# Softmax totals once per pair, three more folded value loads, and re-cut weight loads of the first MLP, in a two-layer decode kernel

## The chip, the cores and the metric

The kernel runs on one core of a Trainium2 chip. The metric is device time in microseconds (us) of one execution; the lower the better. The core has five engines that run their own instruction streams and wait for one another by semaphores: PE (matmul), DVE (vector), ACT (scalar), POOL (GpSimd) and SP, which here does nothing but issue loads. All loads from device memory run on 16 DMA engines that the whole core shares.

## The reference, cut to what matters

The network is a decode step for two sequences (B = 2) with one token each and D = 576 channels. It applies attention, an MLP, the same attention and the same MLP again, each with a layer norm before it and a residual after it:

```python
x = x + A(layernorm(x)); x = x + M(layernorm(x))
x = x + A(layernorm(x)); x = x + M(layernorm(x))

def A(x):            # 32 heads of 128 channels, 8192 cached positions
    q = (x @ wq)                                   # 576 x 4096
    p = softmax(q . k_cache * 128**-0.5)           # k_cache, v_cache: 2 x 32 x 8192 x 128, f32
    return (p . v_cache) @ wo                      # 4096 x 576
def M(x):            # w_gate, w_up: 576 x 4608; w_down: 4608 x 576
    return (gelu_tanh(x @ w_gate) * (x @ w_up)) @ w_down
```

Each cache holds 268.4 MB, and both attentions read both caches; the weights of one attention and one MLP are 50.7 MB. Almost nothing is computed per byte that is read.

## The kernel before, in words

**Items.** An attention goes through 34 items (`ITEMS`): 30 items of two heads of one sequence (`PAIRS`; items 2k and 2k+1 are the same two heads for sequence 0 and 1), and 4 items of a single head (`SINGLE`). The first attention takes them in order 0 to 33, the second in the opposite order. The keys of an item of two heads are one load of 8.39 MB, its values another. In the steady part of an attention one load of keys and one of values come per item.

**Space.** One tile, `space`, holds everything that is loaded. It has six slots of four parts; an item of two heads takes a pair of slots, so three such loads have a place at a time. Behind and over the last slot lies a ring of four places of 9216 bytes per partition. At build time a small allocator (`Arena`) goes through the program in order: each `done(key)` frees a place, and `pump()` then issues the next loads of one fixed list as far as places are free. So the list sets the order of all loads, SP issues them strictly in that order, and each issue waits at run time for the readers of its place.

**Between the attentions.** Five slots hold keys and values of single-head items over the first MLP, so that the second attention needn't load them (`KEYS_HELD`, `VALUES_HELD`). The first MLP therefore lives on the ring of four places alone: each load there, of 1.18 MB, is issued when PE has read the place. The query weights `wq` of the second attention go through the same ring (`of_half`, `half_products`, L621).

**An item's work.** DVE multiplies keys by the query (L744), POOL adds the halves of each row (L773), DVE adds up the rest (L776). `peak` and `highest` (L798 to L810) find the maximum over all partitions by way of PE, `softmax` (L818) writes weights and per-partition totals on ACT, and `total` (L839) adds the totals over partitions by a matmul with ones, for each item, into one of two small PSUM places that take turns with `highest`; `inverse` (L843) takes reciprocals. `values` (L895) runs the weights against the values on PE, 32 matmuls of 512 columns for an item of two heads. For **folded** items, `folds(n)` (L863), the last two of eight parts are first weighed on DVE (`weigh`, L867, L871 and L876) and added down to four rows on POOL (L879), and one matmul (`folded`, L887) takes the place of eight; this happens while the item after the next is worked on, and frees these two parts only then. `gather`, `context` and `divide` (L934) end a pair of items.

**First MLP.** `norm(split=True)` (L545) writes x transposed in blocks of 32 columns, one block for each two rows of every nine (`u` = 0 to 3) and one for the ninth row. `split_products(h)` (L1112) runs once for each half `h` of the 4608 columns: nine ring places of weights, namely four of gate, one with the ninth rows of gate and up, four of up; each place is 8 matmuls of 288 columns (L1120), which PE's records show as 16 passes. `split_rows` (L272) and `split_middle` (L281) load them; `split_middle` issues two loads of 64 partitions into one place. `activate` (L1142) applies the gate. `down` (L290) loads `w_down` in nine ring places: eight with four rows per partition, and one with the ninth row of four groups in two loads (L305); L1183 multiplies them. The second MLP has room and uses large loads.

**Idle products.** `idle_products(n, side)` (L588, matmul at L592) multiplies the identity with itself into a place that nobody reads. With `side` it writes 256 or 512 columns of one half of the accumulator `acc`; without, 128 columns at a time of a small tile.

**The transition.** `plan_second` (L391) lists the loads of the second attention's start: single parts and groups of parts into places that held data frees one by one (`several_parts`, `one`, `half`; the load is L168).

Of the kernel before, what the change touches and what calls it, by code (L numbers as in the profile page):

```python
# [125 lines left out]
def decode_layers(ctx, tc, x_in, kc, vc, wq, wo, wg, wu, wd, out):  # L126
# [154 lines left out]
    def split_middle(h):  # L281

        def transfers(t):
            for g, w in enumerate((wg, wu)):
                rows = w[:, DF // 2 * h:DF // 2 * (h + 1)].rearrange("(m r) w -> m r w", r=NU)
                nc.sync.dma_start(t[g::2, :], rows[:, NU - 1, :])

        weights(("gu", 0, h), DF // 2, None, transfers)

    def down(layer, piece):  # L290

        src = wd.rearrange("(h p r) c -> p h (r c)", h=2, r=2 * NI)
        apart = wd.rearrange("(t p i) c -> p t i c", t=NT, i=NI)

        def transfers(t):
            if layer == 1:
                h, lo, hi = piece
                nc.sync.dma_start(t, src[:, h, lo * D:hi * D])
            elif len(piece) == 3:
                n, lo, hi = piece  # L300
                nc.sync.dma_start(t.rearrange("p (i c) -> p i c", c=D), apart[:, n, lo:hi, :])
            else:
                to = t.rearrange("p (t c) -> p t c", c=D)
                for lo, hi in ((0, 3), (3, NT)):
                    nc.sync.dma_start(to[:, lo:hi, :], apart[:, lo:hi, NI - 1, :])  # L305

        n = piece[2] - piece[1] if len(piece) == 3 else NT
        weights(("d", layer, piece), n * D, whole_at[layer], transfers)
# [12 lines left out]
    def out_rows(layer, g):  # L321
# [17 lines left out]
        [(t, lo, lo + 4) for t in range(NT) for lo in (0, 4)] + [(NI - 1,)],  # L339
        [(0, 0, 18), (1, 0, 9), (1, 9, 15), (1, 15, 17), (1, 17, 18)],  # L340
# [154 lines left out]
    home = consts.tile([P, 3 * DH + 20], F32, name="home")  # L495
# [19 lines left out]
    smalls = [bank2[:, 4 * GH + P + 2 * i:4 * GH + P + 2 * i + 2] for i in range(2)]  # L515
    low = bank2[:, 4 * GH + P + 4:]
# [20 lines left out]
    def small(p, n):  # L537

        if n > 2:
            return turned[0:p, 0:n]  # L540
        smalls.append(smalls.pop(0))
        return smalls[0][0:p, 0:n]


    def norm(split=False, then=None):  # L545
# [13 lines left out]
        if split:  # L559
            xm = xs[:, :5 * 32].rearrange("p (u m e) -> p u m e", u=5, e=2)  # L560
            nc.vector.tensor_scalar(
                xm[:, 0:4], xr[:, 0:NU - 1, :].rearrange("p (u e) m -> p u m e", e=2), mv[:, 0:1], side[:, 0:1],
                op0=ALU.subtract, op1=ALU.mult,
            )
            to, of_x = xm[:, 4], xr[:, NU - 1, :]
            xs = xs[:, :5 * 32].rearrange("p (u q) -> p u q", u=5)
        else:
            to, of_x = xc, x
            xs = xs.rearrange("p (q u) -> p u q", u=NU)
        nc.vector.scalar_tensor_tensor(  # L570
            to, of_x.unsqueeze(2).to_broadcast(list(to.shape)), mv[:, 0:1],
            side.unsqueeze(1).to_broadcast(list(to.shape)), op0=ALU.subtract, op1=ALU.mult,
        )
# [34 lines left out]
    def attention(layer):  # L608
# [12 lines left out]
        def half_products(h):  # L621

            for k in range(4):
# [6 lines left out]
                if k > 0 if h else k < 3:  # L630
                    idle_products(1)
# [207 lines left out]
        def total(n):  # L839
            tot[n] = small(P, 2)  # L840
            nc.tensor.matmul(tot[n][:, :ITEMS[n].heads], ones, rs.pop(n), start=True, stop=True)  # L841

        def inverse(n):  # L843
            it, t = ITEMS[n], tot.pop(n)
            if it.heads == 2:
                rinv[n] = work.tile([P, 2], F32, name="rinv", bufs=4)
                nc.vector.reciprocal(rinv[n], t)
            else:
                if it.h not in of_head:
                    of_head[it.h] = work.tile([P, 2], F32, name="rinv", bufs=4)  # L850
                rinv[n] = of_head[it.h]
                nc.vector.reciprocal(rinv[n][:, it.b:it.b + 1], t[:, 0:1])
# [10 lines left out]
        def folds(n):  # L863

            return 3 <= n < PAIRS - 3
# [68 lines left out]
        def divide(n, by_scalar=False):  # L934
# [11 lines left out]
            for b, i in ((b, i) for b in range(B) for i in range(2)):  # L946
                to = oT[lo + 32 * i:lo + 32 * i + 32, it.h // GH, :, :, b]
                o = po[lo:lo + 32, :, 2 * b + i:2 * b + i + 1].to_broadcast([32, GH, 2])
                ri = rinv[n - it.b + b][lo:lo + 32, i:i + 1]
# [151 lines left out]
    def mlp(layer):  # L1101
# [10 lines left out]
        def split_products(h):  # L1112

            steps = [(("g", layer, h, u), u, 0) for u in range(4)] + [(("gu", layer, h), 4, 0)]
            steps += [(("u", layer, h, u), u, 1) for u in range(4)]
            for key, u, g in steps:
                w = ready.pop(key).rearrange("p (k c w) -> p k c w", c=4, w=HG)
                for k in range(2):
                    for c in range(4):
                        nc.tensor.matmul(  # L1120
                            acc[32 * c:32 * c + 4 * B, h, :HG], window(u, 4 * k + 2 * g), w[:, k, c, :],
                            start=(key == steps[0][0] and k == 0), stop=(key == steps[-1][0] and k == 1),
                        )
# [47 lines left out]
        for n, piece in enumerate(DOWN[layer]):  # L1171
            if n < len(IDLE[layer]):
                idle_products(IDLE[layer][n], 0)
            w = ready.pop(("d", layer, piece)).rearrange("p (i c) -> p i c", c=D)
            if len(piece) == 1:
                rows = [(t // 2, t % 2, NI - 1) for t in range(NT)]
            elif split:
                rows = [(piece[0] // 2, piece[0] % 2, i) for i in range(piece[1], piece[2])]
            else:
                rows = [(r // NI, piece[0], r % NI) for r in range(piece[1], piece[2])]  # L1180
# [7 lines left out]
            done(("d", layer, piece))  # L1188
# [37 lines left out]
```

## Time and profile before

| | |
|---|---|
| three runs | 2683.21, 2681.78, 2683.00 us; median 2683.0 |
| the profiled execution | 2682.85 us |
| its span, first to last instruction | 2681.1 us |
| busy: PE, DVE, ACT, POOL | 909.0, 1989.8, 165.4, 1551.8 us |
| read from device memory | 1152.39 MB, 430 GB/s over the span |
| chain of work that ended last | DMA 67%, DVE 19%, PE 8%, ACT 3%, POOL 2% |

A busy time is a sum over stages that have different limits, so it doesn't say what a stage is worth. The chain of work is followed back from the last instruction: each piece is what released the next one. A DMA piece of the chain runs from the issue of the load to its landing, so it includes the time that the load spent queued behind earlier loads. A row of the stretches view has start and end of a stretch, its length, the busy time of PE, of PE's weight loads, of DVE, ACT and POOL (in brackets the instructions), the granted PE clock, the busy share of the DMA engines and the rate. A row of the time line has start, duration, engine, line, operation and tiles, and in brackets the idle time before it and who ended it.

### The profile page before, as it was taken

The numbers are of one execution on the slowest core, as the hardware profiler recorded it, in microseconds if no ns is written. First come the engines' busy times: TensorE is split into PE (matmuls) and PEld (weight loads), VectorE is DVE, ScalarE is ACT, GpSimd is POOL, SyncE is SP. The second block draws the span as 40 slices with busy tenths as digits, with TensorE's granted clock in tenths as the row PEclk, the third lists the DMA queues.
The fourth block names the chain that finished last, engine by engine and source line by source line (L and its number), as shares of the span: only waits on it lengthen the run. The fifth ranks groups of instructions, "written<-read, shape, count | busy, mean of one in ns | idle before, by whom it ended". The sixth has DMA issues, their size and how long they took to land.

```text
span 2681.1 us, 15549 instructions
## 1 busy us (share of the span) xinstructions
PE 909.0 (34%) x6276; PEld 284.4 (11%) x6276; DVE 1989.8 (74%) x935; ACT 165.4 (6%) x792; POOL 1551.8 (58%) x407
## 2 busy tenths in 40 slices
PE   1323332233223223334663333223222323332346
PEld 0100000000000000111221100000000000000022
DVE  4878888888788878867037778888888888888740
ACT  0000000000000000001026000000000000000000
POOL 2546676667666766744028457666766666676520
PEclk8656655665566566566986665566566556655678
DMA  9999999999999999999999999999999999999998
GB/s 423 438 430 431 435 434 431 434 432 434 434 432 433 434 432 435 429 430 428 416 411 430 436 429 433 434 434 432 430 436 434 431 434 433 434 432 432 435 428 383
DMA packets 29352, 1153.40 MB, mean 430 GB/s; under 512 B 3272, under 2 KB 3296, under 8 KB 4320
## 3 DMA queue, kind: packets, MB, share of 16 engines
q1 hardware_dynamic: 29240, 1152.40, 99.8%
q8 instruction: 49, 0.80, 0.1%
q14 instruction: 23, 0.19, 0.0%
q10 hardware_dynamic: 40, 0.01, 0.0%
HBM read 1152.39 MB, written 0.00 MB: 430 GB/s over the span
## 4 chain that ended last, share of the span: by engine, by line
DMA 67%; DVE 19%; PE 8%; ACT 3%; POOL 2%; issue 1%; SPq 0%; another core or an unknown queue 0%; POOLq 0%; ACTq 0%; DVEq 0%
DMA space<-in_A_k_cache_dram 57%; DVE space L744 17%; PE acc L887 3%; DMA space<-in_A_v_cache_dram 3%; DMA space<-in_B_w_down_dram 2%; POOL space L773 2%; ACT prz L833 2%; DVE scores L776 2%; PE bank L659 1%; DMA space<-in_B_w_up_dram 1%; DMA space<-in_B_w_gate_dram 1%; PE bank L841 1%; PE bank L810 1%; DMA space<-in_A_wo_dram 1%; ACT space L766 0%
## 5 line engine op out<-in xcount | busy, mean ns | idle before, releaser
L773 POOL TENSOR_TENSOR space<-space 128x3072 f32<-128x3072 f32 (+4 forms) x221 | 1128.0, 5104 | 476.3 <-DVE space L744 331.3
L744 DVE TENSOR_TENSOR space<-space,bank 128x6144 f32<-128x6144 f32 (+4 forms) x223 | 1111.8, 4986 | 343.6 <-DMA space<-in_A_k_cache_dram 270.9
L909 PE MATMUL acc<-space,prz 128*16 128x512 f32 (+1 forms) x3328 | 520.0, 790 | 346.4 <-DMA space<-in_A_v_cache_dram 342.3
L776 DVE TENSOR_REDUCE scores<-space 128x48 f32<-128x3072 f32 (+4 forms) x223 | 569.0, 2551 | 90.8 <-POOL space L773 90.6
L879 POOL TENSOR_TENSOR space<-space 128x2048 f32<-128x2048 f32 x144 | 389.8, 2707 | 384.0 <-DVE space L876 360.7
L659 PE MATMUL bank<-qsb,few 4*64 4x128 f32 (+1 forms) x256 | 46.2, 437 | 889.9 <-DVE space L744 881.9
L876 DVE TENSOR_TENSOR space<-space,bank 128x4096 f32<-128x4096 f32 x48 | 212.2, 4420 | 1.8 <-DVE bank L871 0.2
L909 PEld LDWEIGHTS acc<-space,prz 128*16 128x16 f32 (+1 forms) x3328 | 106.4, 118 | 742.0 <-DMA space<-in_A_v_cache_dram 378.7
L825 ACT ACTIVATE nbs<-bank 128x2 f32<-128x2 f32 (+1 forms) x68 | 11.6, 171 | 2010.2 <-PE bank L810 1973.1
L659 PEld LDWEIGHTS bank<-qsb,few 4*64 4x64 f32 (+1 forms) x256 | 20.8, 202 | 909.9 <-DVE space L744 892.0
L581 POOL TENSOR_TENSOR rstd<-ve,few 128x1 f32<-128x1 f32 x4 | 2.2, 550 | 177.0 <-DVE ve L579 177.0
L887 PE MATMUL acc<-space,few 128*16 128x512 f32 x96 | 90.6, 1047 | 0.0
L802 PE MATMUL bank<-ident,m 128*1 128x128 f32 x68 | 20.3, 298 | 196.3 <-DVE m L800 196.1
L1147 DVE STREAM_TRANSPOSE gu<-acc 128x288 f32<-128x288 f32 x4 | 1.9, 483 | 93.4 <-ACT acc L1145 93.4
L841 PE MATMUL bank<-few 128*128 128x2 f32 x120 | 35.3, 363 | 81.4 <-ACT prz L833 81.4
L932 PE MATMUL bank<-few,wide 128*32 128x4 f32 (+1 forms) x272 | 21.8, 203 | 119.3 <-DVE wide L924 119.3
L833 ACT ACTIVATE prz<-scores,nbs 64x128 f32<-64x128 f32 (+1 forms) x128 | 50.7, 396 | 11.7 <-POOL prz L823 8.8
L766 ACT ACTIVATE space<-space 128x128 f32<-128x128 f32 x164 | 48.4, 296 | 19.8 <-DVE space L744 16.7
L810 PE MATMUL bank<-m,few 1*128 1x2 f32 (+1 forms) x136 | 38.5, 350 | 27.4 <-DVE m L808 27.4
L585 DVE TENSOR_TENSOR x<-bank,x 128x144 f32<-128x144 f32 x4 | 1.2, 308 | 59.1 <-PE bank L1183 39.3
L923 DVE TENSOR_TENSOR acc<-acc,few 128x512 f32<-128x512 f32 x34 | 23.1, 680 | 29.2 <-PE acc L909 29.2
L760 POOL TENSOR_TENSOR space<-space,qs 128x512 f32<-128x512 f32 x23 | 29.2, 1272 | 19.7 <-ACT qs L741 19.7
(103 smaller groups left out, 524.2 us busy)
## 6 DMA issues: line engine op xcount, KB each, us to landing
space<-in_A_k_cache_dram SPq DMA_DIRECT2D x6, 4096.0 KB
space<-in_A_v_cache_dram SPq DMA_DIRECT2D x5, 4096.0 KB
space<-in_B_w_gate_dram SPq DMA_DIRECT2D x8, 1152.0 KB
space<-in_B_w_up_dram SPq DMA_DIRECT2D x8, 1152.0 KB
space<-in_B_w_down_dram SPq DMA_DIRECT2D x8, 1152.0 KB
space<-in_A_wq_dram SPq DMA_DIRECT2D x9, 1024.0 KB
space<-in_A_wo_dram SPq DMA_DIRECT2D x2, 4608.0 KB
space<-in_A_v_cache_dram SPq DMA_DIRECT2D x4, 2048.0 KB
```

Source lines behind the costliest of these rows:

```text
L659: nc.tensor.matmul(qb[n][to, :], pick[32 * c:32 * c + 4, r:r + 1].to_broadcast([4, P // it.heads]), qsb[32 * c:32 * c + 4, (h % 4) * DH:(h ...
L744: nc.vector.tensor_tensor(out=u[:, :r, :], in0=t[:, :r, :], in1=qb[n].unsqueeze(1).to_broadcast([P, r, DH]), op=ALU.mult)
L766: nc.scalar.activation(u[:, j, :], u[:, j, :], AF.Copy, accum_out=S[n][:, base(n, k) + j:base(n, k) + j + 1])
L773: nc.gpsimd.tensor_tensor(out=half, in0=half, in1=u[:, :r, DH // 2:], op=ALU.add)
L776: nc.vector.tensor_reduce(out=S[n][:, base(n, k):base(n, k) + own_rows(n, k, m)], in_=prod.pop((n, k)), axis=AX.X, op=ALU.add)
L810: nc.tensor.matmul(mT[n][:, :heads], ones[0:1, :], m1[:, :heads], start=True, stop=True)
L833: nc.scalar.activation(pr[at, lo:].rearrange("p (g e) -> p g e", e=4)[:, 0:it.rows // 2 * it.heads:2 * it.heads, :], s[at, :it.rows].rearr ...
L841: nc.tensor.matmul(tot[n][:, :ITEMS[n].heads], ones, rs.pop(n), start=True, stop=True)
L876: nc.vector.tensor_tensor(out=t, in0=t, in1=share.unsqueeze(2).to_broadcast([P, rows, DH]), op=ALU.mult)
L879: nc.gpsimd.tensor_tensor(out=t[:, :rows - less], in0=t[:, :rows - less], in1=t[:, less:rows], op=ALU.add)
L887: nc.tensor.matmul(accumulator(n)[0:16, :], owner[:, 8 * ITEMS[n].b:8 * ITEMS[n].b + 16], part_at(arena.live[key, lo][0], 4 * DH), start=F ...
L909: nc.tensor.matmul(accumulator(n)[32 * c:32 * c + m, :], pr[:, at:at + m], t[g // 4][:, g % 4 * 4:g % 4 * 4 + 4, :].rearrange("p j d -> p ...
```

## The change

It does these things at once:

- **Totals.** `total` runs one matmul with four columns once per pair of items, when the second item's totals are there, and `inverse` one reciprocal of four columns. `highest` and `total` each have a PSUM place of their own.
- **Folds.** `folds(n)` holds for `layer < n < 27` in place of `3 <= n < 27`: items 1 and 2 of the first attention and item 2 of the second are folded as well.
- **Ninth rows.** The ninth rows of gate come in one load of 128 partitions (row and half of the columns), those of up in another. Both are used behind the eight other places of half 0, for both halves, with 16 matmuls each; half 1 has eight places. `norm` writes two blocks for the ninth row, one for each half, with zeros between, by a memset on POOL and one more operation on DVE. The columns of a half are now taken with a stride of 18.
- **Down.** The rows of `w_down` are dealt to partitions 18 at a time; eight loads of four rows, and a ninth place with two loads of two rows.
- **Idle products.** In `half_products` one of 512 columns in place of two of 128. In `split_products` one of 256 columns in place of two of 128 for most steps of half 1.
- **Transition.** Two groups of `several_parts` are cut 1 + 3 and 1 + 2 parts in place of 2 + 2 and 2 + 1.

```diff
-    def split_middle(h):
+    def split_ninth(name, w):
+
+        rows = w.rearrange("(m r) (s w) -> m r s w", r=NU, s=2)
...
+            nc.sync.dma_start(t, rows[:, NU - 1, :, :])
+
+        weights((name, 0, 0, NU - 1), DF // 2, None, transfers)
...
-        [(t, lo, lo + 4) for t in range(NT) for lo in (0, 4)] + [(NI - 1,)],
-        [(0, 0, 18), (1, 0, 9), (1, 9, 15), (1, 15, 17), (1, 17, 18)],
+        [[(h, lo, lo + 4)] for h in range(2) for lo in range(0, 16, 4)] + [[(h, 16, 18) for h in range(2)]],
+        [[(0, 0, 18)]] + [[(1, lo, hi)] for lo, hi in ((0, 9), (9, 15), (15, 17), (17, 18))],
...
-        for k in range(0, 4, 2):
-            several_parts(("v", 1, SINGLE[0]), vc, SINGLE[0], k, 2, v63, k)
-        for k, m, where, at in ((1, 2, k62, 0), (3, 2, k62, 2), (5, 2, v62, 0), (7, 1, v62, 2)):
+        for k, m in ((0, 1), (1, 3)):
+            several_parts(("v", 1, SINGLE[0]), vc, SINGLE[0], k, m, v63, k)
+        for k, m, where, at in ((1, 2, k62, 0), (3, 2, k62, 2), (5, 1, v62, 0), (6, 2, v62, 1)):
             several_parts(pair, kc, last, k, m, where, at)
...
                 for u in range(4):
                     split_rows("g", wg, h, u)
-                split_middle(h)
                 for u in range(4):
                     split_rows("u", wu, h, u)
+                if h == 0:
+                    split_ninth("g", wg)
+                    split_ninth("u", wu)
...
+            nc.gpsimd.memset(xs[:, 4 * 32 + 1:4 * 32 + 1 + 2 * 31].rearrange("p (e q) -> p e q", e=2)[:, :, 0:31:2], 0.0)
...
+            own = xs[:, 4 * 32:4 * 32 + 2 * 33].rearrange("p (e q) -> p e q", e=2)[:, :, 0:32:2]
+            nc.vector.tensor_scalar(
+                own, xr[:, NU - 1, :].unsqueeze(1).to_broadcast([P, 2, 16]), mv[:, 0:1], side[:, 0:1],
+                op0=ALU.subtract, op1=ALU.mult,
+            )
+            xs = xs[:, :6 * 32].rearrange("p (u q) -> p u q", u=6)
...
                 if k > 0 if h else k < 3:
-                    idle_products(1)
+                    idle_products(2, 1 - h)
...
         def total(n):
-            tot[n] = small(P, 2)
-            nc.tensor.matmul(tot[n][:, :ITEMS[n].heads], ones, rs.pop(n), start=True, stop=True)
+
+            if ITEMS[n].heads == 1:
+                tot[n] = four[:, 0:1]
+                nc.tensor.matmul(tot[n], ones, rs.pop(n), start=True, stop=True)
+            elif completes(seq.index(n)):
+                tot[n] = four
+                nc.tensor.matmul(tot[n], ones, sums.rearrange("p a i -> p (a i)"), start=True, stop=True)
...
-            return 3 <= n < PAIRS - 3
+            return layer < n < PAIRS - 3
...
-            steps = [(("g", layer, h, u), u, 0) for u in range(4)] + [(("gu", layer, h), 4, 0)]
-            steps += [(("u", layer, h, u), u, 1) for u in range(4)]
+            steps = [((name, layer, h, u), u, g) for g, name in enumerate("gu") for u in range(4)]
+            steps += [((name, layer, h, NU - 1), 4, g) for g, name in enumerate("gu") if h == 0]
             for key, u, g in steps:
-                w = ready.pop(key).rearrange("p (k c w) -> p k c w", c=4, w=HG)
+                w = ready.pop(key).rearrange("p (c m k i) -> p k c m i", c=4, k=2, i=NI)
+                for v in range(2) if u == 4 else (h,):
...
                 if key != steps[-1][0]:
-                    idle_products(1, None if h else 1)
+                    idle_products(1, 1 - h if (u < 4 if h == 0 else u) else None)
```

More of the change, by code (lines that the diff above doesn't have):

```diff
@@ L514, in decode_layers @@
     turned = bank2[:, 4 * GH:4 * GH + P]
-    smalls = [bank2[:, 4 * GH + P + 2 * i:4 * GH + P + 2 * i + 2] for i in range(2)]
-    low = bank2[:, 4 * GH + P + 4:]
+    pair, four = bank2[:, 4 * GH + P:4 * GH + P + 2], bank2[:, 4 * GH + P + 2:4 * GH + P + 6]
+    low = bank2[:, 4 * GH + P + 6:]
     share = low[:, :FOLD * JC]
@@ L1112, in split_products @@
         def split_products(h):
-            steps = [(("g", layer, h, u), u, 0) for u in range(4)] + [(("gu", layer, h), 4, 0)]
-            steps += [(("u", layer, h, u), u, 1) for u in range(4)]
+            steps = [((name, layer, h, u), u, g) for g, name in enumerate("gu") for u in range(4)]
+            steps += [((name, layer, h, NU - 1), 4, g) for g, name in enumerate("gu") if h == 0]
             for key, u, g in steps:
-                w = ready.pop(key).rearrange("p (k c w) -> p k c w", c=4, w=HG)
[L1118 to L1123, printed above, removed]
+                w = ready.pop(key).rearrange("p (c m k i) -> p k c m i", c=4, k=2, i=NI)
+                for v in range(2) if u == 4 else (h,):
+                    for k in range(2):
+                        for c in range(4):
+                            nc.tensor.matmul(
+                                acc[32 * c:32 * c + 4 * B, v, :HG], window(u + (v if u == 4 else 0), 4 * k + 2 * g), w[:, k, c],
+                                start=(k == 0 and (key == steps[0][0] if v == h == 0 else u == 4 and g == 0)),
+                                stop=(key == steps[-1][0] and v == h and k == 1),
+                            )
                 done(key)
                 if key != steps[-1][0]:
-                    idle_products(1, None if h else 1)
+                    idle_products(1, 1 - h if (u < 4 if h == 0 else u) else None)
         def all_products():
@@ L1173, in mlp @@
                 idle_products(IDLE[layer][n], 0)
[L1174 to L1180, printed above, removed]
+            w = ready.pop(("d", layer, piece[0])).rearrange("p (i c) -> p i c", c=D)
+            rows = [(h, *divmod(r, NI)) for h, lo, hi in piece for r in range(lo, hi)]
+            if not split:
+                rows = [(v, h, i) for h, v, i in rows]
             for k, (v, e, i) in enumerate(rows):
```

61 lines of the change are left out of this document (23 added, 38 removed).

## The prediction

> **What bounds the kernel now.** I read the page first, then the rates by stretch, then the chain that ended last.
>
> ```profile
> span 2681.1 us, 15549 instructions
> DMA  9999999999999999999999999999999999999998
> GB/s 423 438 430 431 435 434 431 434 432 434 434 432 433 434 432 435 429 430 428 416 411 430 436 429 433 434 434 432 430 436 434 431 434 433 434 432 432 435 428 383
> q1 hardware_dynamic: 29240, 1152.40, 99.8%
> ```
>
> The DMA engines are busy in every fortieth of the span but the last, at 99.8% of it. The bytes stay the same in the change, 1152.40 MB. At 433 GB/s they take 2661.4 us of the 2681.1; the other 20 us are the start, the tail, and the slices around the first MLP (416 and 411). So the change can act in three ways only: raise the rate in a stretch, leave the DMA engines without a load, or move the tail. The stretches:
>
> ```profile
> 600.00:1000.00 400.00, 116.79 (x630) 32.75 (x630) 327.33 (x122) 16.72 (x70) 268.76 (x63) 0.59 1.00 433
> 1312.00:1318.00 6.00, 2.73 (x34) 0.85 (x34) 0.25 (x1) 0.47 (x1) 0.00 (x0) 1.00 1.01 422
> 1318.00:1326.00 8.00, 6.96 (x60) 2.72 (x60) 1.40 (x8) 0.23 (x1) 0.00 (x0) 0.57 1.01 416
> 1359.00:1366.00 7.00, 4.81 (x86) 2.14 (x84) 0.00 (x0) 0.00 (x0) 0.00 (x0) 1.00 1.03 409
> 1376.00:1390.00 14.00, 11.64 (x68) 3.62 (x69) 5.94 (x4) 3.55 (x19) 3.33 (x3) 0.63 1.01 401
> 1404.00:1410.00 6.00, 1.59 (x14) 0.40 (x6) 5.06 (x6) 5.37 (x36) 6.00 (x6) 1.00 0.95 351
> 1424.00:1452.00 28.00, 16.38 (x106) 4.90 (x97) 23.74 (x27) 19.64 (x129) 22.21 (x17) 0.76 1.01 431
> ```
>
> The steady attention runs at 433 with DVE and POOL idle a fifth and a third of the time. The first MLP, whose runs are of 9216 bytes, reaches 422 where nothing is in its way. Against 422, 1318 to 1326 loses 0.11 us (8 x 6/422), 1359 to 1366 loses 0.22, and 1376 to 1390 loses 0.70; against the 431 of later key loads, 1404 to 1410 loses 1.11. Together that is 2.1 us, the most that the touched stretches can give back. What covers a late release is the queue:
>
> ```profile
> 464.05 27.15 DMA space<-in_A_k_cache_dram
> 1319.04 2.14 PE acc L1120 x16
> 1366.91 10.41 DMA space<-in_A_wq_dram
> 1377.37 1.89 PE acc L616 x8
> 2531.84 48.47 DMA space<-in_A_v_cache_dram
> ```
>
> A DMA row of the chain runs from issue to landing. A load of keys (8.39 MB, 19.4 us at 433) landed 27.15 us after its issue, so it stood 7.8 us behind the load before; a release late by less costs nothing. A 1.05 MB load of `wq` (2.5 us at 422) took 10.41, so its cover is 7.9 us.
>
> **The change, part by part.**
>
> ```profile
> L841 PE MATMUL bank<-few 128*128 128x2 f32 x120 | 35.3, 363 | 81.4 <-ACT prz L833 81.4
> L909 PE MATMUL acc<-space,prz 128*16 128x512 f32 x3072 | 476.8, 786 | 337.6 <-DMA space<-in_A_v_cache_dram 337.6
> ```
>
> Totals: 60 matmuls (two passes each, hence x120) become 30, which takes half of the 35.3 us from PE, along with 30 small reciprocals on DVE. PE waits for loads around them, as the 337.6 us in front of L909 show; 0 on the end. The total now waits for the second item's softmax, but its only reader, `divide`, runs an item later; should that cover be gone, DVE would wait for one matmul, 0.4 us.
>
> Folds: the three items are priced by the last fold of the second attention and by what stands around the new one, item 2's.
>
> ```profile
> 2495.17 4.42 DVE L876 TENSOR_TENSOR space<-space,bank 128x4096 f32<-128x4096 f32 x1
> 2499.67 8.28 POOL L879 TENSOR_TENSOR space<-space 128x2048 f32<-128x2048 f32 x3 [7.83 <-DVE space L876]
> 2512.57 1.89 PE L887 MATMUL acc<-space,few 128*16 128x512 f32 x2
> 2531.43 0.80 SPq L168 DMA_DIRECT2D space<-in_A_v_cache_dram  x2
> 2531.56 0.28 DVE L800 TENSOR_REDUCE m<-scores 128x1 f32<-128x128 f32 x1
> 2541.64 2.29 DVE L744 TENSOR_TENSOR space<-space,bank 128x2048 f32<-128x2048 f32 x1 [9.79 <-DMA space<-in_A_k_cache_dram]
> 2544.06 4.74 POOL L773 TENSOR_TENSOR space<-space 128x1024 f32<-128x1024 f32 x2 [14.85 <-DVE space L744]
> 2575.69 0.17 DVE L847 RECIPROCAL rinv<-bank 128x2 f32<-128x2 f32 x1 [2.35 <-PE bank L841]
> ```
>
> A fold adds 4.4 us on DVE, 8.3 on POOL, 1.9 on PE, and takes 8 matmuls of two passes from PE. In the first attention it makes items 1 and 2 like every later one: the load into their slots is released later than now and keeps the steady 7.8 us of cover. Item 2 of the second attention folds behind L800, in the 9.79 us in which DVE waits for the last keys: DVE is done at about 2536.5, POOL at 2544.8, PE at 2546.7. Two things wait behind it. POOL's additions for item 0 start 0.7 us later, and the values of item 0, issued now at 2531.9 on freed places, are issued at about 2547. That load landed at 2580.3 (2531.84 + 48.47), so its own transfer began near 2560.9: 14 us of cover. Item 0's softmax was finished at 2575.9, 4.4 us ahead of that landing, which covers the 0.7. The loads of `wo` behind it in SP's queue wait for the values of item 1, which land later than 2547. Cost 0; without cover, the issue's delay of 15 us would count in full.
>
> First MLP:
>
> ```profile
> 1293.12 0.24 DVE L570 SCALAR_TENSOR_TENSOR xc<-x,mv,few 128x32 f32<-128x32 f32 x1
> 1293.47 0.35 DVE L575 STREAM_TRANSPOSE xt<-xc 128x160 f32<-128x160 f32 x1
> 1295.09 0.50 SPq L286 DMA_DIRECT2D space<-in_B_w_gate_dram  x1
> 1296.16 1.16 PE L1120 MATMUL acc<-space,xt 128*8 128x288 f32 x16 [0.72 <-DMA space<-in_B_w_gate_dram]
> 1297.14 0.59 PE L592 MATMUL acc<-ident 128*4 128x256 f32 x2
> L1120 PE MATMUL acc<-space,xt x288: 402/406/687, 1293.9 to 1342.0; 128*8 128x288 f32 x144
> L1136 PE MATMUL acc<-space,xt x288: 421/436/687, 2616.9 to 2655.7; 128*8 128x288 f32 x144
> ```
>
> The norm keeps its count on DVE's path, with a transpose a fifth longer (0.07 us); the memset is on an idle POOL. The first product is at most 0.3 us later and so is the fifth load, issued at 1295.09; PE then waits 0.72 us for weights, so this is hidden. The second MLP already reads its weights with the stride of 18: 436 ns at the median against 406, so a place takes 1.25 in place of 1.16 us. A load arrives every 2.8 us (1.18 MB at 422). The ninth places have 16 matmuls, 2.5 us, and with an idle product 3.1: two steps in a row 0.3 us too long, made up in the next, where PE would otherwise wait. 0; the bound is +0.6. Bytes and run lengths of the ninth rows stay. The last `down` place goes from 512 runs of 2304 bytes to 256 of 4608: -0.2 us, the loss of 1359 to 1366, of which I take all. That the dip of the clock at 1318 (0.57, a step of 2.14 us) goes, because half 0 now ends with PE fuller, is worth 0.1 at most; I take 0.
>
> Query weights:
>
> ```profile
> 1368.22 1.02 PE L592 MATMUL acc<-ident 128*4 128x512 f32 x2
> 1372.26 0.60 PE L592 MATMUL bank<-ident 128*4 128x128 f32 x4
> 1379.03 1.06 PE L592 MATMUL bank<-ident 128*4 128x128 f32 x4
> 1319.04 1.63 PE L1120 MATMUL acc<-space,xt 128*8 128x288 f32 x12 [1.93 <-DVE ga L1158]
> ```
>
> Six idle products of 0.60 us become 1.02. At full clock a step is then 1.04 + 1.02 = 2.1 us, under the 2.5 in which a load arrives. In 1376 to 1390 the granted clock was 0.63 and the product took 1.89 us, releases came late and the rate fell to 401. If the fuller PE keeps the clock, part of the 0.70 us comes back. The bounds are -0.7 and, at half clock (1.80 us for an idle product of 512, scaled by 1.06/0.60, so 0.74 more in each of six steps), +4.4 against a cover of some 8. I take -0.4. Here a rule speaks against the change. The Trainium skill ("TensorE: Matmul & The Clock Gate", Part 1) says that the clock falls after an idle window of about 3.4 us and returns after a busy one. By it PE never idles long enough here, the idle products buy nothing, and the sum would be 0.4 us less of a gain. This case's trace differs: the last row above shows no gap over 1.93 us, and the clock was at half in 1318 to 1326 all the same.
>
> Transition:
>
> ```profile
> 1403.63 2.04 SPq L168 DMA_DIRECT2D space<-in_A_v_cache_dram  x2
> 1400.04 5.24 PE L909 MATMUL acc<-space,prz 128*8 128x512 f32 x32 [0.82 <-ACT qs L741]
> ```
>
> The load issued at 1403.63 waited for two parts that PE frees one after the other (a quarter of L909's time, 1.3 us, each at that clock). With one part first, it is issued about 1 us earlier, in front of the stretch of 351 GB/s. The second load's issue stays, with the first's 1 MB ahead of it in place of 2: 2.4 us less of cover, none of it needed if the queue holds. Between 0 and -1.1 I take -0.5. The cut 1 + 2 likewise is 0. The Trainium skill ("DMA: Bandwidth & Descriptors", Latency and other measured facts) gives 0.6 us to the first byte of a load issued from SP. If that were all, the old issue was in time and this term is 0. No run here shows that figure by itself; the 351 speaks for a loss around this issue.
>
> **The sum**, on the profiled execution's 2682.85 us (0.15 below the median of the runs shown): -0.2 - 0.4 - 0.5 = -1.1, all else hidden. That is 2681.75, forecast as 2681.8.
>
> **The rivals.**
>
> *Hidden anyway.* The slow stretches are not from late issues, and the terms are 0: 2682.8. For it: the DMA share stays at 1.01 in 1376 to 1390. Against it: 0.95 in 1404 to 1410.
>
> *The gate closes on a fuller PE.* The 4.4 us of longer idle products delay the query and the releases of the ring, the cover doesn't hold at a stage where DVE is busy 23.74 of 28 us, and all of it counts: 2687.3. For it: 0.63 in that stretch. Against it: the clock was full at 1312 to 1318 with PE busy under half.
>
> *The ninth rows' load runs on fewer engines.* Its nest is 64 rows by 2 halves. Were it dealt out by the 2, two engines of 16 would carry 2.36 MB at 54 GB/s, 43.6 us in place of 5.5; the ring would stand still, and less some 8 us of cover 30 us are lost: 2713. It decides from four engines down, where the two loads take 21.8 us and 8.3 are lost; with five it is 4.0. Against it: `split_rows` moves the same nest, and 1312 to 1318, with nothing else in flight, has 422.
>
> *The whole dip goes.* In the slices of 416 and 411 (67 us each, 1273 to 1408) 6.0 us are missing against 433: 2676.8. Against it: the run lengths stay.
>
> **How the numbers follow.** The forecast has 0.57, with its own range 2680.0 to 2682.8 (the gains at their bounds less the 0.7 us by which the runs spread, and the sum without the last two terms); hidden anyway 0.24; the closing gate or steps late in the ninth places 0.11; fewer engines or another stop of the ring over 5.4 us 0.05; the whole dip 0.03. The range from 2679.0 to 2687.0 leaves out the last two and a little of the gate. A measurement of this kernel can tell about 0.2%, 5.4 us, from no change: faster 0.03, same 0.92, slower 0.05.
>
> **What would show it.** Steps are right if the steady stretches stay at 433, the values of the second attention's last item are issued near 2547 and land near 2580, 1376 to 1390 rises above 401 with a clock above 0.63, 1404 to 1410 rises above 351, and products of a ninth place take near 2.5 us. It is wrong if a stretch behind 1310 drops below 400, if PE's weights wait is gone before the products of half 1, or if the last landing moves without any of this, which would mean that the tail of the DMA engines decides.

## The result, and the profile after

| | before | after |
|---|---|---|
| median | 2682.62 us (6 runs, 2681.64 to 2683.56) | 2692.01 us (6 runs, 2691.33 to 2693.66) |
| ratio | | 1.0036, 95% interval 1.0023 to 1.0049 |
| the profiled execution, its span | 2682.85, 2681.1 us | 2691.51, 2689.7 us |

The change makes the kernel 9.4 us slower, in place of the 1.1 us of gain that were forecast; 2692.01 lies outside the range of 2679.0 to 2687.0. The page of after has these four lines beside those of before:

```profile
span 2689.7 us, 15386 instructions
DMA  9999999999999999989999999999999999999998
GB/s 421 436 435 435 426 437 432 434 435 431 434 431 433 434 432 435 433 362 426 422 419 425 433 435 437 433 431 433 432 432 436 434 431 434 433 432 435 431 431 382
q1 hardware_dynamic: 28952, 1152.40, 99.4%
```

The bytes are the same. One slice of forty stands out: the eighteenth, 1143 to 1210 us, has 362 GB/s where before has 430; no other differs by more than 9. So the time was not lost where most of the change lies (the first MLP and the transition, behind 1290), but at the end of the first attention's two-head items. In steps of 10 us there (columns: start and end, length, busy PE, PE's weight loads, DVE, ACT, POOL, granted PE clock, DMA share, GB/s), first before:

```profile
1160.00:1170.00 10.00, 0.66 (x9) 0.56 (x8) 9.96 (x6) 1.04 (x4) 9.30 (x2) 0.50 0.90 387
1170.00:1180.00 10.00, 9.31 (x64) 1.97 (x64) 8.51 (x3) 0.00 (x0) 6.04 (x2) 0.77 1.02 439
```

and after:

```profile
1160.00:1170.00 10.00, 0.69 (x12) 0.67 (x16) 9.97 (x5) 1.04 (x4) 9.32 (x2) 0.50 0.65 282
1170.00:1180.00 10.00, 8.61 (x64) 1.96 (x63) 8.52 (x3) 0.00 (x0) 5.80 (x2) 0.84 0.30 106
```

The compute engines do nearly the same in both; the DMA engines run dry. (387 - 282) x 10 us and (439 - 106) x 10 us are 4.4 MB, 10.1 us at 433. Over the whole trace, taking the time at which the same number of bytes has landed, after stands 0.0 us behind before at 500 MB, 10.5 at 510 MB, 8.9 at 600 MB and 8.6 at the end. So one hole makes the whole difference, and a little is given back behind it.

Why the engines ran dry is seen in SP's time line (start, duration, engine, line, tiles, loads issued). Before:

```profile
1141.75 0.38 SPq L168 DMA_DIRECT2D space<-in_A_k_cache_dram  x1
1142.18 37.60 SPq L168 DMA_DIRECT2D space<-in_A_v_cache_dram  x2
```

After:

```profile
1140.51 0.33 SPq L168 DMA_DIRECT2D space<-in_A_v_cache_dram  x1
1176.68 0.33 SPq L168 DMA_DIRECT2D space<-in_A_k_cache_dram  x1
1180.45 0.81 SPq L168 DMA_DIRECT2D space<-in_A_v_cache_dram  x2
```

The load of keys in the first row of before, of item 30 (`SINGLE[0]`), is issued 35 us later, and as SP issues strictly in order, nothing else goes out between 1140.51 and 1176.68. What SP waited for in this stretch of after (us in total, times, longest), and the chain of work there (start, duration, what):

```profile
SPq L168 <- DVE scores L774: 26.2, 1, 26.2
SPq L168 <- DMA space<-in_A_k_cache_dram: 15.7, 2, 9.6
```

```profile
1165.72 3.34 DVE scores L774
1169.06 4.33 DVE space L742
1173.39 3.27 DVE scores L774
1176.66 0.02 issue
1176.68 12.17 DMA space<-in_A_k_cache_dram
1188.88 2.30 DVE space L742
```

(Line numbers of after are two or three off those of before; L774 adds up the scores.) SP waits first for the landing of item 29's keys, until 1150.45 (the 9.6 us), then for DVE's adding up of this item, the last one of two heads (the 26.2 us). The load that goes out then has half the size of one for two heads: 4.19 MB, 9.7 us at 433. It lands after 12.17, so next to nothing stands before it, and DVE waits for it.

### The profile page after: what moved, and what is told of

The parts are those of the page before. It is cut to its first block, busy times and chain, and to the rows that moved or that the text cites. A ratio compares the mean times of both kernels' runs of the same rounds, so it can differ in the third digit from the quotient of the medians.

```text
span 2689.7 us, 15386 instructions
## 1 busy us (share of the span) xinstructions
PE 886.0 (33%) x6184; PEld 269.2 (10%) x6184; DVE 2001.9 (74%) x911; ACT 165.6 (6%) x792; POOL 1576.8 (59%) x417
## 4 chain that ended last, share of the span: by engine, by line
DMA 65%; DVE 21%; PE 8%; POOL 3%; ACT 2%; issue 2%; another core or an unknown queue 0%; SPq 0%; POOLq 0%; ACTq 0%; DVEq 0%
DMA space<-in_A_k_cache_dram 58%; DVE space L742 18%; PE acc L890 3%; DMA space<-in_B_w_down_dram 3%; DMA space<-in_B_w_gate_dram 2%; DVE scores L774 2%; POOL space L771 2%; PE bank L657 1%; DMA space<-in_B_w_up_dram 1%; PE bank L808 1%; ACT prz L831 1%; DMA space<-in_A_wo_dram 1%; PE bank L844 1%; ACT space L764 0%; PE acc L912 0%
## 5 line engine op out<-in xcount | busy, mean ns | idle before, releaser
L882 POOL TENSOR_TENSOR space<-space 128x2048 f32<-128x2048 f32 x153 | 414.4, 2708 | 408.5 <-DVE space L879 392.5
L774 DVE TENSOR_REDUCE scores<-space 128x48 f32<-128x3072 f32 (+4 forms) x223 | 568.7, 2550 | 93.6 <-POOL space L771 93.5
L912 PE MATMUL acc<-space,prz 128*16 128x512 f32 (+1 forms) x3280 | 506.9, 782 | 352.6 <-DMA space<-in_A_v_cache_dram 348.4
L879 DVE TENSOR_TENSOR space<-space,bank 128x4096 f32<-128x4096 f32 x51 | 225.4, 4421 | 2.0 <-DVE bank L874 0.3
L890 PE MATMUL acc<-space,few 128*16 128x512 f32 x102 | 96.4, 1049 | 0.8 <-POOL space L882 0.8
L935 PEld LDWEIGHTS bank<-few,wide 128*32 128x32 f32 x272 | 19.1, 154 | 216.2 <-issue 211.1
L954 ACT ACTIVATE oT<-bank,rinv 32x8 f32<-32x8 f32 x108 | 28.1, 260 | 190.1 <-PE bank L935 189.1
```

What stands on the lines that cost most here:

```text
L774: nc.vector.tensor_reduce(out=S[n][:, base(n, k):base(n, k) + own_rows(n, k, m)], in_=prod.pop((n, k)), axis=AX.X, op=ALU.add)
L879: nc.vector.tensor_tensor(out=t, in0=t, in1=share.unsqueeze(2).to_broadcast([P, rows, DH]), op=ALU.mult)
L882: nc.gpsimd.tensor_tensor(out=t[:, :rows - less], in0=t[:, :rows - less], in1=t[:, less:rows], op=ALU.add)
L890: nc.tensor.matmul(accumulator(n)[0:16, :], owner[:, 8 * ITEMS[n].b:8 * ITEMS[n].b + 16], part_at(arena.live[key, lo][0], 4 * DH), start=F ...
L912: nc.tensor.matmul(accumulator(n)[32 * c:32 * c + m, :], pr[:, at:at + m], t[g // 4][:, g % 4 * 4:g % 4 * 4 + 4, :].rearrange("p j d -> p ...
L935: nc.tensor.matmul(po[lo:lo + 32, i, :c], t[:, i::GH], of[:, :c], start=True, stop=True)
```

## The theory and its rivals

**Place.** `plan_first` writes out by hand where the first loads behind the two-head items go:

```python
        k(SINGLE[0], (0,))
        half(("v", 0, last), vc, last, 0, 1)
        half(("v", 0, last), vc, last, 4, 5)
        k(SINGLE[1], (3,))
```

The two-head items are placed by `Arena.pair`, which tries the three pairs of slots in the order in which they were freed. A fold frees the values' pair an item later, so the load that would have taken it takes another pair, and a later load gets this one. After that, who takes turns with whom stays shifted until another release changes the order. Going through the allocator's code in program order (no view of the profile shows slots) gives:

| slots of | keys of 28 | keys of 29 | values of 28 |
|---|---|---|---|
| before | 0, 1 | 2, 3 | 4, 5 |
| after | 4, 5 | 0, 1 | 2, 3 |

So the keys of item 30, written to slot 0, had to wait for the readers of item 28's keys, and now wait for those of item 29's. What the trace does show is the moment in which two loads change places. Before, at item 2 (PE's products of item 1's values, DVE's adding up of item 2, SP):

```profile
123.09 8.86 PE L909 MATMUL acc<-space,prz 128*16 128x512 f32 x64 [9.69 <-DMA space<-in_A_v_cache_dram]
130.02 2.29 DVE L776 TENSOR_REDUCE scores<-space 128x32 f32<-128x2048 f32 x1 [1.48 <-POOL space L773]
132.03 0.33 SPq L168 DMA_DIRECT2D space<-in_A_v_cache_dram  x1
132.44 0.39 SPq L168 DMA_DIRECT2D space<-in_A_k_cache_dram  x1
```

After:

```profile
130.27 2.29 DVE L774 TENSOR_REDUCE scores<-space 128x32 f32<-128x2048 f32 x1 [1.47 <-POOL space L771]
132.59 0.33 SPq L168 DMA_DIRECT2D space<-in_A_v_cache_dram  x1
150.43 1.89 PE L890 MATMUL acc<-space,few 128*16 128x512 f32 x2
152.35 0.33 SPq L168 DMA_DIRECT2D space<-in_A_k_cache_dram  x1
```

Before, the values' load went out as PE ended with item 1's values (131.95) and the keys' load as DVE ended with item 2's keys (132.31). After, the values' load goes out as DVE ends (132.56), and the keys' load 20 us later, behind the fold's matmul (152.32). The two have swapped pairs.

**Rivals.** *Work:* the added 4.4 us on DVE and 8.3 on POOL in each fold make the attention late. *Elsewhere:* the totals, the ninth rows or the idle products change the timing, and the hole is only where it shows. By place, the hole comes and goes with the slots alone, whatever the number of folds.

## The experiments

Times are medians, with the lowest and highest run; a ratio is against runs of before on the same chip, with its 95% interval. Each kernel is the one named, before or after, but for the edit shown.

**The folds alone**, in before:

```diff
-            return 3 <= n < PAIRS - 3
+            return layer < n < PAIRS - 3
```

> The kernel before with one line changed: folds(n) holds for layer < n < 27. Place theory (the early folds shift which pair of slots every later load takes, so that the keys of item 30, whose slot 0 is written by hand, lie under the keys of item 29): the whole loss is here, 2691 to 2694 us, the keys of item 30 issued near 1177 us in place of 1142, and a stretch of some 10 us with few loads behind 1160. Rival (the totals once per pair, or another part, hold up the end of the two-head items): 2682 to 2684 us, as before.

Measured: 2693.0 us (2691.71 to 2693.99), 1.0036 [1.0023, 1.0049]. The hole is there, in the row of the stretch and in SP's row for the keys of item 30:

```profile
1170.00:1180.00 10.00, 9.67 (x64) 1.95 (x64) 8.51 (x3) 0.00 (x0) 5.88 (x2) 0.73 0.29 98
```

```profile
1176.83 0.33 SPq L168 DMA_DIRECT2D space<-in_A_k_cache_dram  x1
```

**All but the folds**, in after:

```diff
-            return layer < n < PAIRS - 3
+            return 3 <= n < PAIRS - 3
```

> The changed kernel with folds(n) for 3 <= n < 27 as before. Place theory: the loss is gone, 2680 to 2683 us, and what is left of the change is its small terms (the prediction's sum of -1.1; the trace of the changed kernel gives back 1.9 us behind the stall). Rival (another part): 2691 to 2694 us.

Measured: 2682.35 us (2681.39 to 2683.77), 0.9998 [0.9989, 1.0007]; the same stretch is full:

```profile
1170.00:1180.00 10.00, 9.78 (x64) 2.28 (x64) 8.52 (x3) 0.00 (x0) 5.90 (x2) 0.72 1.01 433
```

These two put the whole loss on the folds: *elsewhere* is out. They don't part *place* from *work*.

**The slots alone**, in before, without any new fold: the hand-written slots 0 and 1 change names with 2 and 3, so that the keys of item 30 lie under those of item 29, as in after.

```diff
-        k(SINGLE[0], (0,))
-        half(("v", 0, last), vc, last, 0, 1)
+        k(SINGLE[0], (2,))
+        half(("v", 0, last), vc, last, 0, 3)
...
-        k(SINGLE[1], (3,))
+        k(SINGLE[1], (1,))
...
-        k(SINGLE[2], (2,))
+        k(SINGLE[2], (0,))
...
-        k(SINGLE[3], (0,))
+        k(SINGLE[3], (2,))
...
-        v(SINGLE[2], (3,))
+        v(SINGLE[2], (1,))
...
-        places[v63] = [SLOT + k * PART for k in range(4)]
+        places[v63] = [3 * SLOT + k * PART for k in range(4)]
...
-        cache(("v", 1, last), vc, last, (0, 1))
+        cache(("v", 1, last), vc, last, (2, 3))
```

> The kernel before with no part of the change; only the slots written by hand are renamed, 0 with 2 and 1 with 3, so that the keys of item 30 want the slot under the keys of item 29. Place theory: as slow as the change, 2690 to 2694 us, with the keys of item 30 issued near 1177 us. Rival (folds or another part cost by themselves): 2682 to 2684 us, as before.

Measured: 2692.43 us (2691.97 to 2693.12), 1.0034 [1.0021, 1.0047]. SP's row and the stretch are those of after:

```profile
1176.72 0.33 SPq L168 DMA_DIRECT2D space<-in_A_k_cache_dram  x1
```

```profile
1170.00:1180.00 10.00, 8.88 (x64) 1.75 (x56) 8.51 (x3) 0.00 (x0) 5.78 (x2) 0.80 0.29 98
```

No instruction is added here (both traces have 15549), so *work* isn't needed for the loss.

**The early folds kept, slots back**, in after: items 1 and 2 of the first attention are folded, 25 and 26 are not, which shifts the turns back before the end. That makes 24 folds there, as many as in before and two fewer than in after, so this run tells about when an item is folded, not about how many are.

```diff
-            return layer < n < PAIRS - 3
+            return 0 < n < PAIRS - 5 if layer == 0 else 2 <= n < PAIRS - 3
```

> The changed kernel with its three folds kept and items 25 and 26 of the first attention not folded. By the allocator's rule these two put the rotation back, so that the keys of 28 lie in slots 0-1 and those of 29 in 2-3. Place theory: the change's loss is gone with its own folds in place, 2681 to 2684 us, keys of item 30 issued near 1141. Rival (items 1 and 2 are folded too early, and their lateness is carried along to the end of the two-head items): 2690 us or more.

Measured: 2684.12 us (2682.76 to 2684.83), 1.0003 [0.9994, 1.0012], 0.1 us above what was expected, and not told apart from before. The hole is gone with the two early folds in place:

```profile
1160.00:1170.00 10.00, 0.61 (x8) 0.56 (x8) 9.97 (x5) 1.03 (x4) 9.24 (x2) 0.50 0.90 387
1170.00:1180.00 10.00, 9.88 (x64) 2.23 (x64) 8.52 (x3) 0.00 (x0) 5.99 (x2) 0.71 1.01 436
```

**Which fold**, in after: in the first attention only item 2, or only item 1, is folded beside 3 to 26.

```diff
-            return layer < n < PAIRS - 3
+            return 2 <= n < PAIRS - 3
```

> The changed kernel with only item 2 folded beyond the folds of before (in both attentions). By the allocator's rule the keys of item 29 and the values of 28 change places (slots 4-5 and 2-3), but slots 0-1 stay under the keys of item 28. Place theory: the keys of item 30 and half of the values of item 29 are issued near 1142 us as before, the other half waits for the keys of 29 a microsecond longer under 19 us of queued loads, so no loss: 2681 to 2684 us. Rival (any early fold, or any shift of the slots, costs): 2686 us or more.

```diff
-            return layer < n < PAIRS - 3
+            return (n == 1 or n > 2) and n < PAIRS - 3 if layer == 0 else 2 <= n < PAIRS - 3
```

> The changed kernel with only item 1 folded beyond the folds of before in the first attention (and item 2 in the second). By the allocator's rule slots 0-1 are then under the values of item 28, which PE reads from 1170 us on. Place theory: the keys of item 30 are issued when half of these values are read, near 1175 us, almost as late as in the change, 2689 to 2693 us, though only one fold was added to the first attention. Rival (a loss that grows with the number of folds): about half of the change's loss, 2686 to 2688 us.

Item 2 alone: 2682.29 us (2681.44 to 2684.0), 0.9997 [0.9988, 1.0006], the keys of item 30 issued at 1141.35. Item 1 alone: 2691.38 us (2690.01 to 2692.62), 1.0031 [1.0018, 1.0043]. Its row:

```profile
1176.48 0.33 SPq L168 DMA_DIRECT2D space<-in_A_k_cache_dram  x1
```

One fold more costs nothing or 8.3 us, by which item it is: the same work, another turn. With item 1 alone slot 0 lies under item 28's values, by the allocator's rule, and SP waits for PE in place of DVE, with nearly the same time.

**Two other folds**, in after: items 0 and 2.

```diff
-            return layer < n < PAIRS - 3
+            return (n != 1 if layer == 0 else n > 1) and n < PAIRS - 3
```

> The changed kernel with items 0 and 2 of the first attention folded in place of 1 and 2: as many folds, as much work on DVE, POOL and PE, values released as late. By the allocator's rule this leaves the pairs of slots at the end of the two-head items as before the change (keys of 28 in slots 0-1, of 29 in 2-3). Place theory: 2680 to 2683 us, keys of item 30 issued near 1142. Rival (the folds' own work or the later release of early values costs): 2690 us or more.

Measured: 2684.84 us (2682.83 to 2686.36), 1.0006 [0.9997, 1.0014]. The hole at 1170 doesn't come (keys of item 30 at 1143.47) with as many folds as in after, but the time lies between the two forecasts, 1.8 us above that by place. The interval doesn't tell it from before; the trace shows a loss at 100 to 110 us, where the rate of before is 426: (426 - 315) x 10 us is 1.1 MB, 2.6 us at 433. This run's row of the stretch, and behind it DVE, PE and SP in its time line:

```profile
100.00:110.00 10.00, 0.37 (x1) 0.08 (x1) 9.39 (x5) 0.00 (x0) 2.46 (x1) 0.50 0.81 315
```

```profile
99.61 2.29 DVE L774 TENSOR_REDUCE scores<-space 128x32 f32<-128x2048 f32 x1 [1.41 <-POOL space L771]
101.92 0.33 SPq L168 DMA_DIRECT2D space<-in_A_v_cache_dram  x1
116.93 1.89 PE L890 MATMUL acc<-space,few 128*16 128x512 f32 x2
118.85 0.33 SPq L168 DMA_DIRECT2D space<-in_A_k_cache_dram  x1
```

In before these two loads go out at 93.55 (the end of PE's products of item 0) and 102.03 (the end of DVE's adding up). It is the same swap, two items earlier. There 8.4 us more before the values' load aren't covered: the DMA share falls from 0.98 to 0.81.

**Four folds, and the slots follow**, in after: items 0, 1 and 2 folded, with the slots renamed as in the third experiment.

```diff
-            return layer < n < PAIRS - 3
+            return (layer == 0 or n > 1) and n < PAIRS - 3
...
-        k(SINGLE[0], (0,))
+        k(SINGLE[0], (2,))
```

> The changed kernel with item 0 folded too, and the slots written by hand renamed (0 with 2, 1 with 3) so that they follow where the allocator then has the keys of items 28 and 29. Place theory: no wait at 1142 to 1177, so no loss of 9 us; what stays are the 2 us that folding item 0 cost near 105 us in the run with items 0 and 2: 2683.5 to 2686 us. Rival (more folds, more loss): over 2692 us.

Measured: 2683.76 us (2682.74 to 2685.63), 1.0005 [0.9996, 1.0014]; the keys of item 30 go out at 1143.25. The renaming that cost 9 us in before doesn't cost it here: neither the slots' names nor the number of folds makes the hole, only their pairing does. The start has the loss of item 0's fold again, 322 GB/s in 100 to 110.

**The transition alone**, in before, cut 1 + 3 and 1 + 2, and **the idle products of the query weights alone**, in before:

```diff
-        for k in range(0, 4, 2):
-            several_parts(("v", 1, SINGLE[0]), vc, SINGLE[0], k, 2, v63, k)
-        for k, m, where, at in ((1, 2, k62, 0), (3, 2, k62, 2), (5, 2, v62, 0), (7, 1, v62, 2)):
+        for k, m in ((0, 1), (1, 3)):
+            several_parts(("v", 1, SINGLE[0]), vc, SINGLE[0], k, m, v63, k)
+        for k, m, where, at in ((1, 2, k62, 0), (3, 2, k62, 2), (5, 1, v62, 0), (6, 2, v62, 1)):
```

> The kernel before with the loads of the transition cut 1 + 3 and 1 + 2 in place of 2 + 2 and 2 + 1, and nothing else. If the slow stretch came from the late issue at 1403.6 us, the rate of 1404 to 1410 rises from 351 to over 420 GB/s and the bytes behind it land about 1 us earlier: 2681 to 2683 us. If it came from something else, the stretch stays near 351: 2682 to 2684 us.

```diff
-                    idle_products(1)
+                    idle_products(2, 1 - h)
```

> The kernel before with idle products of 512 columns in half_products, and nothing else. Prediction's term: the granted clock of 1376 to 1390 us rises from 0.63 to about 1 and the rate from 401 towards 422 GB/s, worth 0.4 us: 2681.5 to 2683.5 us. Rival (the gate closes on a fuller PE): the clock stays near 0.6, steps take 3.7 us, 2684 to 2688 us.

Measured: 2683.11 us (2681.66 to 2684.0), 0.9999 [0.999, 1.0008], and 2682.7 us (2681.49 to 2683.64), 0.9998 [0.9989, 1.0006]. Each kernel's two stretches that the prediction spoke of, the transition alone first:

```profile
1376.00:1390.00 14.00, 8.16 (x67) 2.59 (x68) 7.51 (x6) 4.83 (x27) 3.93 (x3) 1.00 1.00 409
1404.00:1410.00 6.00, 1.47 (x14) 0.40 (x6) 4.59 (x5) 5.37 (x37) 6.00 (x6) 1.00 1.03 430
```

```profile
1376.00:1390.00 14.00, 10.25 (x60) 1.90 (x60) 7.29 (x6) 4.83 (x27) 3.93 (x3) 1.00 1.01 413
1404.00:1410.00 6.00, 1.96 (x18) 0.57 (x10) 4.80 (x5) 5.37 (x36) 6.00 (x6) 0.78 1.03 422
```

Both stretches are better than in the profile of before (401 at a clock of 0.63, and 351), in both kernels. Each kernel changes only one of the two, so the other got better without an edit. The folds alone and the slots alone have neither edit, and there the same stretches, 9 us later, have 418 and 418 in the first, 415 and 414 in the second. The clock of 0.63 and the 351 are in these stretches of no other profile here. A rate near 401 is: all but the folds, which has both edits, has a full clock and hardly more:

```profile
1376.00:1390.00 14.00, 10.28 (x58) 1.90 (x60) 7.35 (x6) 4.83 (x27) 3.94 (x3) 1.00 1.00 404
```

Item 2 alone, with both edits too, has 401 at a clock of 0.88. No gain can be put down to either edit.

## Why the prediction was wrong, step by step

**What bounds the kernel** was read rightly: the bytes are fixed, and the time is lost where the DMA engines have no load.

**Folds in the first attention, the step that failed.** It said: "In the first attention it makes items 1 and 2 like every later one: the load into their slots is released later than now and keeps the steady 7.8 us of cover", and priced it at 0. This much held: the keys' load went out 20 us later and landed 29.04 us after its issue, 9.6 more than its 19.4 of transfer, at 181.39, where in before DVE had these keys at 181.11; and the steady rate stayed:

```profile
152.35 29.04 DMA space<-in_A_k_cache_dram
```

```profile
600.00:1000.00 400.00, 114.69 (x620) 31.31 (x620) 327.21 (x117) 16.74 (x70) 268.88 (x63) 0.59 1.00 433
```

But a later release also changes which load takes the place, and 26 items on, a hand-written slot met the wrong one. There one issue was late by 35 us, against loads in the queue that lasted into 1160 to 1170. The term was 0 and measured +9.8 (the folds alone, with all three). The forecast looked at the wait that was moved, not at the order of places that the wait decides. "Another stop of the ring" shared a chance of 0.05 with the fewer engines, but none of the rivals was this mechanism, and the rival on the slow side, the gate, had nothing to do with it. The sentence on what would prove it wrong looked only behind 1310, and took a last landing that moves without such a stretch for the tail of the DMA engines; it moved by 8.6 us, and the hole is at 1170.

The signs that were named for being right all came, and none of them looked at the end of the first attention. Two came by luck: after has 412 GB/s at a clock of 0.88 in the stretch of the query weights and 442 in that of the transition (9 us later than in before), but kernels without these edits lie above 401, 0.63 and 351 there too.

**Item 2's fold in the second attention** went as worked out. With after's 8.6 us taken off, the values of the last item are issued at 2547.3 (forecast 2547) and land at 2580.3 (forecast 2580):

```profile
2554.00 1.89 PE L890 MATMUL acc<-space,few 128*16 128x512 f32 x2 [0.82 <-POOL space L882]
2555.92 0.33 SPq L168 DMA_DIRECT2D space<-in_A_v_cache_dram  x1
2588.85 9.19 PE L912 MATMUL acc<-space,prz 128*16 128x512 f32 x64 [3.23 <-DMA space<-in_A_v_cache_dram]
```

The landing hasn't moved, though the issue has by 15 us: the cover held. Here the prediction did ask which load takes the places that the fold holds, the step that it left out in the first attention. The kernel with item 2 folded in both attentions measured 0.9997.

**Totals**: half of PE's 35.3 us went, and the kernel without the folds, which has this, measured 0.9998, not told apart from before:

```profile
L844 PE MATMUL bank<-few 128*128 128x4 f32 x60 | 17.6, 364 | 38.7 <-ACT prz L831 38.7
```

**Ninth rows**: the products of a ninth place take 2.27 us (forecast 2.5), those of another 1.23 (1.25). The rate through both loads stays at the ring's 422, so the rival of fewer engines is refuted. The second ninth place (1327.95) starts without a wait; from 1333.51 on PE waits for weights again, 0.47 us and then 1.14, so the lateness is made up, as forecast:

```profile
1325.16 2.27 PE L1124 MATMUL acc<-space,xt 128*8 128x288 f32 x32 [1.14 <-DMA space<-in_B_w_gate_dram]
1331.39 1.23 PE L1124 MATMUL acc<-space,xt 128*8 128x288 f32 x16 [1.17 <-DVE gu L1152]
```

```profile
1316.00:1326.00 10.00, 5.76 (x70) 1.89 (x74) 0.00 (x0) 0.00 (x0) 0.00 (x0) 1.00 1.01 423
1326.00:1336.00 10.00, 7.41 (x98) 2.67 (x90) 1.65 (x8) 0.71 (x2) 0.00 (x0) 1.00 1.01 422
```

The dip of the clock at 1318 goes, as forecast. 1318 to 1326 has a clock of 1.00 in three kernels with the new ninth places (all but the folds, slots back, item 2 alone), against 0.57, 0.79 and 0.79 in three with the old ones (before, the transition alone, the idle products alone). The rates there don't follow the clock: 421, 412, 417 against 416, 422, 415.

**Last `down` place**, -0.2: in the same six kernels 1359 to 1366 has 414, 418, 414 with the new cut and 409, 410, 409 with the old one. So this dip does come back, and the new cut gains 0.08 to 0.15 us there at most. It is too small for the times to show.

**Query weights and transition**, -0.4 and -0.5: both were read from dips of a single execution, and neither is shown by the runs. The first took the slow clock for the cause of the slow rate; with the clock full the rate was 404 (all but the folds). The second took the late issue for the cause of the 351; with the old cut the idle products alone issued that load at 1403.44, in before it was 1403.63, and the stretch had 422. All the small terms together were -1.1, and the kernel without the folds measured 0.9998 [0.9989, 1.0007], which holds -1.1 and 0 alike; "hidden anyway" fits these parts at least as well. The upper end of the forecast's own range, 2682.8, is 2682.65 by its own rule (the sum without the last two terms); nothing hangs on it.

The Trainium skill ("TensorE: Matmul & The Clock Gate", Part 1) has the clock fall after an idle window of about 3.4 us. No gap of PE from 1362 to 1390 in before is over 2.01 us, so by this rule the longer idle products buy nothing. This case's trace agrees in that the clock was 1.00 in 1376 to 1390 without them (the transition alone). It differs in that the clock fell to 0.63 there in before, and to 0.57 in 1318 to 1326, where the prediction's row shows a gap of 1.93 us. The Trainium skill ("DMA: Bandwidth & Descriptors", Latency and other measured facts) gives 0.6 us to the first byte, and if that were all, the old issue at the transition was in time. This case's trace agrees in that the stretch had 422 with the old cut.

No version here is faster than before by more than the interval: the best are 0.9997 and 0.9998.

**Left open:** why a dip comes in one execution and not in another, and whether the small terms are worth some tenths of a microsecond. The slots come from the allocator's code, which places the loads at build time; the runs confirm what it says of who waits, and no trace shows the addresses themselves.

## What to carry to other kernels

Where places are handed out in the order in which they come free, and some are fixed by hand, delaying one release is two changes: a later issue, and another order of who follows whom, which can surface a thousand microseconds on. So after pricing the wait, go through the allocator to the next hand-written place and name whose reader it then waits for. And a dip that is to be won back should be there in a second profile before it becomes a term.

## What the runs showed that was not expected

- An issue 20 us late, at 152 us, left no mark on the rate of after around it, as the values' load ahead of it was still under way (PE got these values at 162.16); one 35 us late, at 1176, put the bytes behind it 10.5 us back. In the row of the stretch around the first:

```profile
140.00:160.00 20.00, 3.63 (x16) 1.47 (x16) 16.68 (x6) 2.19 (x9) 16.25 (x5) 0.50 1.03 446
```

- A stretch of 14 us with the same code ran at a granted clock of 0.63 and 401 GB/s in one execution (before) and at 1.00 and 409 in another (the transition alone), while the two kernels' medians differ by 0.0 us (2683.1 and 2683.11).
